# Attention chunks of groups 2 to 5 served two at a visit, in a fused attention and MLP kernel

## The chip, the cores and the metric

The kernel runs on one core of a Trainium2 chip. The metric is the device time of one execution in microseconds (us), lower is better. The core's engines each run their own instruction queue in order and meet through semaphores: TensorE (PE, with its weight loads PEld), VectorE (DVE), ScalarE (ACT), GpSimd (POOL) and SyncE (SP). SP and POOL issue the DMAs here. PE writes into PSUM, which the kernel uses as eight banks of 128 partitions x 512 floats.

## The reference

Attention with a decay for each head, over 4 batches, 8 heads, 768 positions and a head size of 64, in blocks of 64 positions with a running state; its output, as 3072 tokens of 512, goes through an MLP with an exact GELU and a hidden size of 2048.

```python
for b in range(nb):                                   # blocks of 64 positions
    intra = einsum('bhic,bhjc->bhij', qb, kb) * Dmask  # lam**(i-j) where i >= j
    intra = einsum('bhij,bhjd->bhid', intra, vb)
    inter = einsum('bhid,bhde->bhie', qb * lam_pow, kv_state)
    out[:, :, sl] = intra + inter
    kv_state = lam_block * kv_state + einsum('bhsd,bhse->bhde', kb * rev_pow, vb)
x = out.transpose(0, 2, 1, 3).reshape(3072, 512)
h = x @ w_in
return (0.5 * h * (1 + erf(h / sqrt(2)))) @ w_out
```

## The kernel before

**Chunks and groups.** The kernel takes 128 positions at a time. Chunk n is positions 128 (n // 4) onwards of batch n % 4, all eight heads; there are 24 chunks. Four chunks, one of each batch at the same positions, are a group of 512 tokens; there are six groups, 0 to 5. The MLP works on one group while attention prepares the next, so "in group 1" means: while the MLP of group 1 runs and chunks 8 to 11 are prepared.

**What a chunk needs.**

- Loads of k, q and v (`load`, line 67), issued by POOL, cast on the way from float32 to bf16. `prefetch` keeps them four chunks ahead of the scores; the buffers (10 for k, 8 for q and v) come free when the older chunk has been used.
- `begin` and `dma_transposes` (lines 188 and 189): SP issues two DMA transposes, k to kT and q to qT. Both have three buffers, so those of chunk n wait for chunk n - 3: kT for its scores, qT for the first part of its outputs.
- `decay_v` (line 163): POOL scales v by powers of the decay, into v_dec (7 buffers).
- `scores` (line 196): eight matmuls on PE, each on 64 of the array's 128 rows, into two banks of the tag "sc"; then `masked` (line 204) on DVE, two multiplications by the causal mask, PSUM to SBUF (sc_m).
- `outputs`: the part from the states (line 226, four matmuls on the whole array) and the part from the values (line 231, eight matmuls on 64 of the array's columns) into the bank "o"; then DVE scales it into x_t (line 241), the MLP's input.
- `next_state` (line 211): four matmuls into the bank "t", and two DVE operations (lines 218 and 219), once in each group for each of its own chunks.

**The MLP.** In groups 1 to 5 it is 30 blocks of about equal length. Blocks 0 to 15 each make one slice of 128 hidden units (four matmuls of 512 columns into a bank "mh", line 412, then GELU on ACT, line 416). Blocks 16 to 29 multiply by w_out in seven products of half size, two blocks each, in the order m3, m4, m5, m2, m1, m6, m7 (sixteen matmuls for two blocks, line 306). m3, m4, m5 and m2 take a bank "mo" each in turn, m1 takes two "mh" (called s and r), m6 writes s and m7 adds to r. DVE forms sums of the inputs (g_sum, line 281) and of the results; SP stores the two halves of a group's output after m6 and m7 (line 316). The tags sc, mh and mo have two banks each, o and t one.

**The order.** It is written out by hand. PE, DVE, ACT, POOL and SP get their instructions in the order in which the Python code calls for them. The list `todo` holds pairs of a place and a step: place(g + f) is a share f of group g's blocks, and a step runs before the first block whose start is at or after its place. In the kernel before, chunk i of the next group (i from 0 to 3) has its scores at 0.21 + 0.2 i in group 1 and at 0.06 + 0.245 i in groups 2 to 4; its outputs at the place of the next chunk's scores, just ahead of them, and those of the last chunk at 0.93; its `begin` 0.32 ahead of its scores (0.28 for chunk 8). So a visit is outputs of one chunk, then scores of the next. The states of a group's own chunks stand at 0.01, 0.12, 0.18 and 0.24.

Of the kernel before, what the change touches and what calls it, by code (L numbers as in the profile page):

```python
# [8 lines left out]
F32 = mybir.dt.float32  # L9
BF16 = mybir.dt.bfloat16  # L10
# [5 lines left out]
def kernel(  # L16
# [23 lines left out]
    M = 4  # L40
    NG = NCH // M
# [7 lines left out]
    work_pool = ctx.enter_context(tc.tile_pool(name="work", bufs=3))  # L49
# [115 lines left out]
    def transposed(c, name, tag, empty):  # L165

        src, t_ps = getattr(c, name), bank([128, HP, C], BF16, tag, "t_ps")
        for hp in range(HP):
            nc.tensor.transpose(t_ps[:, hp, :], src[:, 2 * hp:2 * hp + 2, :], ident)  # L169
        dst = work_pool.tile([128, HP, C], BF16, tag=name + "T", name=name + "T")  # L170
        setattr(c, name + "T", dst)
        empty(dst, t_ps)  # L172

# [3 lines left out]
    def transposes(c):  # L177
        if c.early:
            transposed(c, "k", "mo", nc.scalar.copy)
            transposed(c, "q", "mo", nc.vector.tensor_copy)  # L180
        else:
            transposed(c, "k", "mh", nc.scalar.copy)
            transposed(c, "q", "mh", scaled)

    def dma_transposes(c):
        c.kT = work_pool.tile([128, HP, C], BF16, tag="kT", name="kT")
        c.qT = work_pool.tile([128, HP, C], BF16, tag="qT", name="qT")
        nc.sync.dma_start_transpose(out=c.kT, in_=c.k.rearrange("p h d -> p (h d)"))
        nc.sync.dma_start_transpose(out=c.qT, in_=c.q.rearrange("p h d -> p (h d)"))

    def scores(c):
        sc_ps = [bank([128, HP, C], F32, "sc", f"sc_ps{hi}") for hi in range(2)]
        for hp in range(HP):
            for hi in range(2):
                p = slice(hi * D, (hi + 1) * D)
                nc.tensor.matmul(sc_ps[hi][:, hp, :], c.kT[p, hp, :], c.qT[p, hp, :], start=True, stop=True)  # L196
        c.sc_m = work_pool.tile([128, HP, 2, C], BF16, tag="sc_m", name="sc_m")
        c.sc_ps = sc_ps
        for hi in range(0 if c.n == 0 else 2):
            masked(c, hi)  # L200

    def masked(c, hi):
        mask = decay[:, hi] if c.early else cmask[:, None, :].to_broadcast((128, HP, C))
        nc.vector.tensor_mul(c.sc_m[:, :, hi, :], c.sc_ps[hi], mask)  # L204

    def next_state(c):
        if c.sb == NB - 1:
            return
        kv_ps = bank([128, HP, 128], F32, "t", "kv_ps")
        for hp in range(HP):  # L210
            nc.tensor.matmul(kv_ps[:, hp, :], c.k[:, 2 * hp:2 * hp + 2, :], c.v_dec[:, 2 * hp:2 * hp + 2, :],  # L211
                             start=True, stop=True)
        new = work_pool.tile([128, HP, 128], BF16, tag="state_f", name="state", bufs=8)
        if c.sb == 0:
            nc.vector.tensor_mul(new, kv_ps, lam_blk)
        else:
            tmp = work_pool.tile([128, HP, 128], F32, tag="tmp", name="tmp")
            nc.vector.tensor_add(tmp, kv_ps, states[c.n])  # L218
            nc.vector.tensor_mul(new, tmp, lam_blk)  # L219
        states[c.n + M] = new  # L220

    def outputs(c, x_t, off, evacuate=True):
        o_ps = bank([128, HP, C], F32, "o", "o_ps")
        if c.sb > 0:
            for hp in range(HP):
                nc.tensor.matmul(o_ps[:, hp, :], states[c.n][:, hp, :], c.qT[:, hp, :],  # L226
                                 start=(hp == 0), stop=False, skip_group_check=True)
        v = c.v if c.early else c.v_dec
        for hi in range(2):
            for hp in range(HP):  # L230
                nc.tensor.matmul(o_ps[hi * D:(hi + 1) * D, hp, :], v[:, 2 * hp + hi, :], c.sc_m[:, hp, hi, :],  # L231
                                 start=(c.sb == 0 and hp == 0), stop=True, skip_group_check=True)
        c.x_o, c.o_ps = x_t[:, :, off * C:(off + 1) * C], o_ps
        if evacuate:
            empty_outputs(c)

    def empty_outputs(c):
        if c.n < 2 * M:
# [222 lines left out]
    live = {}  # L461
# [10 lines left out]
    def early(n):  # L472
        live[n] = begin(n, early=True)
        return live[n]
# [9 lines left out]
    c = early(0)  # L484
# [4 lines left out]
    causal(1)  # L489
    keep_warm(2)  # L490
    scores(c)
    for hi in range(2):
        masked(c, hi)
# [5 lines left out]
    outputs(live[0], xT[0], 0)  # L499
# [5 lines left out]
    outputs(live[1], xT[0], 1)  # L505
    c = early(2)
    transposed(c, "k", "mh", copy)
    transposed(c, "q", "mo", copy)
# [31 lines left out]
    x1 = lambda n: outputs(live[n], xT[1], n - M)  # L540
# [4 lines left out]
    e = N1  # L545
    group0 = {
        1: [lambda: scores(live[2])],
        5: [lambda: outputs(live[2], xT[0], 2)],
        6: [lambda: next_state(live[0])],
        7: [lambda: next_state(live[1])],  # L550
        8: [lambda: both_transposed(live[3])],
        9: [lambda: next_state(live[2])],
        10: [lambda: scores(live[3])],
        12: [lambda: outputs(live[3], xT[0], 3)],
        17: [lambda: next_state(live[3])],
        e: [w_out_sums, lambda: decay_v(live[4], nc.vector)],
        e + 8: [lambda: transposes(live[4])],
        e + 9: [lambda: scores(live[4])],
        e + 10: [lambda: x1(4), lambda: transposes(live[5])],
        e + 11: [lambda: scores(live[5])],  # L560
        e + 12: [lambda: x1(5), lambda: transposes(live[6])],
        e + 13: [lambda: scores(live[6])],
        e + 14: [lambda: x1(6), lambda: transposes(live[7])],
        e + 15: [lambda: scores(live[7])],
    }
# [10 lines left out]
    todo.sort()  # L576

    def step(minus_kind, n):
        kind = -minus_kind
        if kind == BEGIN:  # L580
            live[n] = begin(n)
            dma_transposes(live[n])
            decay_v(live[n], nc.gpsimd)
        elif kind == SCORES:
            scores(live[n])
            prefetch(n + M)
        elif kind == STATE:
            next_state(live[n])
        else:
            outputs(live[n], xT[n // M], n % M)  # L590

    done = 0
    for g in range(NG):
        if g + 1 < NG:
            alloc_x(g + 1)
        for i, (run, cost) in enumerate(mlp_blocks(g)):
            if g == 0:
                for act in group0.get(i, []):
                    act()
            while todo and todo[0][0] <= done:  # L600
                step(*todo.pop(0)[1:])
            run()
            done += cost
        for item in [t for t in todo if t[2] // M == g + 1 and t[1] != -STATE]:
            todo.remove(item)
            step(*item[1:])


# [28 lines left out]
```

## Time and profile before

| what | value |
|---|---|
| median of three runs | 209.67 us (209.66 to 209.96) |
| the profiled execution | 209.99 us |
| its span, first to last instruction | 208.2 us |
| granted TensorE clock, mean | 0.998 |
| group 1 begins, group 2, group 3, group 4 | 53.50, 84.87, 115.96, 147.06 us |
| h blocks (line 412), matmuls of 512 columns | 75.3 us in 318, start to start 0.216 us |
| scores (line 196) | 9.5 us in 192 |
| outputs (lines 226 and 231, groups 1 to 5) | 7.7 us in 80 and 9.3 us in 160 |
| masks of groups 1 to 5 (line 204) | 25.6 us in 40 |
| kT and qT by DMA, issue to landing | least 2.4, median 5.8 and 5.2, most 8.3 and 9.0 us |

The span is what the profiler saw from the first to the last instruction; the time of the execution has some 1.8 us around it. [...] DMA landings are told by semaphores.

### The profile page before, as it was taken

The numbers are of one execution on the slowest core, as the hardware profiler recorded it, in microseconds if no ns is written. First come the engines' busy times: TensorE is split into PE (matmuls) and PEld (weight loads), VectorE is DVE, ScalarE is ACT, GpSimd is POOL, SyncE is SP. The second block draws the span as 40 slices with busy tenths as digits, with TensorE's granted clock in tenths as the row PEclk, the third lists the DMA queues.
The fourth block names the chain that finished last, engine by engine and source line by source line (L and its number), as shares of the span: only waits on it lengthen the run. The fifth ranks groups of instructions, "written<-read, shape, count | busy, mean of one in ns | idle before, by whom it ended". The sixth has DMA issues, their size and how long they took to land.

```text
span 208.2 us, 4142 instructions
## 1 busy us (share of the span) xinstructions
PE 200.3 (96%) x1708; PEld 130.5 (63%) x1725; DVE 139.0 (67%) x220; ACT 81.7 (39%) x145; POOL 97.1 (47%) x112
## 2 busy tenths in 40 slices
PE   7889999999999999999999999999999999999992
PEld 2457574465555788654688554688555688544881
DVE  4744525855476789889779689579678579123482
ACT  4966563324555410265420265410365410466200
POOL 8999953799998995499300493000200000000000
PEclk9999999999999999999999999999999999999999
DMA  5999999999999999999930699100651000500014
GB/s 116 155 174 177 200 207 188 154 215 148 151 177 154 153 150 154 233 141 175 155 25 3 219 134 175 29 0 3 227 103 29 0 0 3 201 0 0 3 50 151
DMA packets 102370, 24.65 MB, mean 118 GB/s; under 512 B 92880, under 2 KB 99536, under 8 KB 102352
## 3 DMA queue, kind: packets, MB, share of 16 engines
q0 software_dynamic: 80688, 13.37, 90.2%
q1 hardware_dynamic: 21664, 11.02, 23.5%
q8 instruction: 13, 0.21, 0.4%
q14 instruction: 5, 0.04, 0.1%
HBM read 27.27 MB, written 6.29 MB: 161 GB/s over the span
## 4 chain that ended last, share of the span: by engine, by line
PE 86%; POOL 8%; DVE 3%; issue 1%; POOLq 0%; DVEq 0%
PE h_ps L412 39%; PE p_ps L306 9%; PE r_ps L306 8%; PE q_ps L306 8%; PE o_ps L426 7%; PE o_ps L231 4%; PE s_ps L306 3%; PE sc_ps L196 3%; PE kv_ps L211 3%; POOL w_in_t L88 3%; PE o_ps L226 2%; POOL k_t L67 2%; POOL q_t L67 2%; POOL v_t L67 2%; PE t_ps L169 1%
## 5 line engine op out<-in xcount | busy, mean ns | idle before, releaser
L416 ACT ACTIVATE g_t<-h_ps 128x512 bf16<-128x512 f32 (+2 forms) x101 | 58.2, 576 | 81.2 <-PE h_ps L412 81.0
L412 PE MATMUL h_ps<-x_t,w_in_t 128*128 128x512 bf16 (+3 forms) x446 | 88.7, 343 | 0.6
L412 PEld LDWEIGHTS <-w_in_t 128*128 128x128 bf16 x460 | 40.2, 98 | 36.0 <-issue 0.6
L163 POOL TENSOR_TENSOR v_dec<-v_t,lam_m 128x512 bf16<-128x512 bf16 x23 | 25.2, 1101 | 44.5 <-PE kv_ps L211 42.9
L306 PEld LDWEIGHTS <-g_sum 128*128 128x128 bf16 x400 | 38.6, 98 | 5.2
L281 DVE TENSOR_TENSOR g_sum<-g_t 128x1024 bf16<-128x1024 bf16 x50 | 33.6, 716 | 11.3 <-ACT g_t L416 11.3
L204 DVE TENSOR_TENSOR sc_m<-sc_ps,cmask 128x512 bf16<-128x512 f32 x40 | 25.6, 680 | 2.0 <-PE sc_ps L196 2.0
L67 POOL DMA_DIRECT2D v_t<-in_v_dram x24 | 21.4, 893 | 3.3 <-DMA w_out_t<-in_moe_w_out_dram 2.9
L67 POOL DMA_DIRECT2D k_t<-in_k_dram x24 | 22.2, 924 | 1.7 <-DMA w_out_t<-in_moe_w_out_dram 1.4
L67 POOL DMA_DIRECT2D q_t<-in_q_dram x24 | 21.6, 898 | 2.1 <-DMA w_out_t<-in_moe_w_out_dram 2.1
L306 PE MATMUL r_ps<-w_sum,g_sum 128*128 128x256 bf16 x160 | 19.3, 273 | 0.1
L241 DVE TENSOR_TENSOR x_t<-o_ps,lam_q 128x512 bf16<-128x512 f32 x16 | 11.0, 687 | 10.2 <-PE o_ps L231 10.2
L306 PEld LDWEIGHTS <-g_t 128*128 128x128 bf16 x160 | 15.3, 98 | 3.2
L218 DVE TENSOR_TENSOR tmp<-kv_ps,state 128x512 f32<-128x512 f32 x16 | 11.0, 689 | 7.8 <-PE kv_ps L211 7.8
L426 PE MATMUL o_ps<-w_out_t,g_t 128*128 128x512 bf16 x61 | 14.8, 380 | 0.1
L219 DVE TENSOR_TENSOR state<-tmp,lam_blk 128x512 bf16<-128x512 f32 x16 | 14.4, 901 | 0.5
L306 PE MATMUL p_ps<-w_sum,g_t 128*128 128x256 bf16 x80 | 10.1, 273 | 0.0
L196 PE MATMUL sc_ps<-qT,kT 64*128 64x128 bf16 x192 | 9.5, 218 | 0.3 <-DVE qT L172 0.3
L306 PE MATMUL q_ps<-w_sum,g_t 128*128 128x256 bf16 x80 | 9.7, 273 | 0.0
L470 PE MATMUL idle_ps<-idle 128*128 128x256 bf16 (+1 forms) x33 | 8.4, 393 | 1.2 <-DVE idle L101 1.2
L426 PEld LDWEIGHTS <-g_t 128*128 128x128 bf16 x64 | 5.8, 98 | 6.1
L306 PE MATMUL p_ps<-w_out_t,g_sum 128*128 128x256 bf16 x80 | 9.6, 273 | 0.0
(65 smaller groups left out, 168.0 us busy)
## 6 DMA issues: line engine op xcount, KB each, us to landing
out_dram<-o_sb SPq DMA_DIRECT2D x9, 512.0 KB, 2.8
k_t<-in_k_dram POOLq DMA_DIRECT2D x24, 128.0 KB, 5.9
q_t<-in_q_dram POOLq DMA_DIRECT2D x24, 128.0 KB, 6.1
v_t<-in_v_dram POOLq DMA_DIRECT2D x24, 128.0 KB, 6.2
w_out_t<-in_moe_w_out_dram POOLq DMA_DIRECT2D x4, 512.0 KB, 11.1
w_in_t<-in_moe_w_in_dram POOLq DMA_DIRECT2D x7, 256.0 KB, 7.5
out_dram<-o_sb SPq DMA_DIRECT2D x5, 256.0 KB, 5.7
wide_w<-in_moe_w_in_dram SPq DMA_DIRECT2D x1, 512.0 KB, 4.2
```

Source lines behind the costliest of these rows:

```text
L67: nc.gpsimd.dma_start(raw[n, name], chunk_of(name, n))
L163: eng.tensor_mul(c.v_dec, c.v, lam_m[:, :, None].to_broadcast((128, H, D)))
L196: nc.tensor.matmul(sc_ps[hi][:, hp, :], c.kT[p, hp, :], c.qT[p, hp, :], start=True, stop=True)
L204: nc.vector.tensor_mul(c.sc_m[:, :, hi, :], c.sc_ps[hi], mask)
L218: nc.vector.tensor_add(tmp, kv_ps, states[c.n])
L219: nc.vector.tensor_mul(new, tmp, lam_blk)
L241: nc.vector.tensor_mul(c.x_o, c.o_ps, lam_q)
L281: nc.vector.tensor_tensor(gsum[i][:, ks, :], g_t[:, ka + k:ka + k + n4, ta], g_t[:, kb + k:kb + k + n4, tb], op=op)
L306: nc.tensor.matmul(o, left[i](k, slice(u * C, (u + 1) * C)), right[i](k), start=(begin and k == 0), stop=(k == KH - 1), skip_group_check=True)
L412: nc.tensor.matmul(h_ps[:, k, lo:hi], w_in_t[:, ki, (kf + k) * 128:(kf + k + 1) * 128], x_t[:, ki, cols.start + lo:cols.start + hi], start ...
L416: nc.scalar.activation(g_t[:, kf:kf + ks, cols], h_ps, ACT.Gelu)
L426: nc.tensor.matmul(om[io], g_t[:, kf, io * C:(io + 1) * C], w_out_t[:, kf, :], start=(kf == 0), stop=(kf == NK2 - 1))
```

## The change

Nothing is computed in another way: the same matmuls, masks and transfers are called in another order and into other banks.

- `visit(when, done, asked, banks, masks)` replaces the separate steps. It runs the outputs of up to two chunks (`done`): the part from states for both, then the part from values for both, then both evacuations. The second chunk's outputs go to the bank "t". Then it runs the scores of up to two further chunks (`asked`): the first in "sc", the second in "mo" (in "mh" at one visit); the masks of the second chunk come first, unless `masks` gives each of the four masks a place of its own.
- In group 1 there is a visit before block 8 (scores of 8 and 9), one before block 20 (outputs of 8 and 9, scores of 10 and 11) and one before block 26 (outputs of 10 and 11, scores of 12 and 13, which belong to group 3). In groups 2 and 3 there is a visit before block 9 (outputs of the group's first two chunks, scores of the other two) and one before block 26 (outputs of these, scores of the first two of the group after). In group 4 they are the same without the scores of the last.
- At the visits before block 26 the masks stand at blocks 26 and 28 and at blocks 1 and 2 of the next group.
- The begins move: chunk 8 stays at 0.93 of group 0; 9, 10 and 11 stand at 1.0, 1.13 and behind the visit before block 8 of group 1; 12 and 13 at 1.57 and 1.60; and in the later groups the last two chunks at 0.0 and 0.04, the first two of the group after at 0.57 and 0.60.
- qT has four buffers in place of three.

```diff
-        qT = work_pool.tile([128, HP, C], BF16, tag="qT", name="qT")
+        qT = work_pool.tile([128, HP, C], BF16, tag="qT", name="qT", bufs=4)
...
-    def outputs(c, x_t, off, evacuate=True):
-        o_ps = bank([128, HP, C], F32, "o", "o_ps")
+    def from_states(c, tag):
+        c.o_ps = bank([128, HP, C], F32, tag, "o_ps")
...
+    def outputs(*chunks):
+
+        for c, tag in zip(chunks, ("o", "t")):
+            from_states(c, tag)
+        for c in chunks:
+            from_values(c)
+        for c in chunks:
             empty_outputs(c)
...
-    BEGIN, STATE, SCORES, OUTPUTS = 0, 1, 2, 3
-    todo = [(total, -OUTPUTS, 2 * M - 1)]
-    for n in range(2 * M, NCH):
-        g, i = n // M - 1, n % M
-        first, apart = (0.21, 0.2) if g == 1 else (0.06, 0.245)
-        at = first + apart * i
-        todo += [(place(g + at - (0.28 if n == 2 * M else 0.32)), -BEGIN, n), (place(g + at), -SCORES, n),
-                 (place(g + (at + apart if i < M - 1 else 0.93)), -OUTPUTS, n)]
-    todo += [(place(n // M + (0.01, 0.12, 0.18, 0.24)[n % M]), -STATE, n) for n in range(M, NCH - M)]
...
+    def begin_at(when, n):
+        def run():
             live[n] = begin(n)
             dma_transposes(live[n])
             decay_v(live[n], nc.gpsimd)
...
+    def visit(when, done, asked, banks="mo mo", masks=None):
+
+        def run():
+            outputs(*[live[n] for n in done])
+            for n, tags in zip(asked, ("sc sc", banks)):
+                scores(live[n], tags, mask=False)
+            if masks is None:
+                for n in reversed(asked):
+                    for hi in range(2):
+                        masked(live[n], hi)
+            for n in asked:
+                prefetch(n + M)
+        at(when, run)
+        if masks:
+            for w, (n, hi) in zip(masks, [(n, hi) for n in asked for hi in range(2)]):
+                at(w, lambda n=n, hi=hi: masked(live[n], hi))
+
+    B = 1 / (NK2 + 14)
+    for g in range(1, NG - 1):
+        n = (g + 1) * M
+        for i, w in enumerate((0.01, 0.12, 0.18, 0.24)):
+            at(g + w, lambda i=i, g=g: next_state(live[g * M + i]))
+        if g == 1:
+            for i, w in enumerate((-0.07, 0.0, 0.13)):
+                begin_at(g + w, n + i)
+            visit(g + 8 * B, [], [n, n + 1])
+            begin_at(g + 8 * B, n + 3)
+            visit(g + 20 * B, [n, n + 1], [n + 2, n + 3], banks="mh mh")
         else:
+            for i in (2, 3):
+                begin_at(g + (i - 2) * 0.04, n + i)
+            visit(g + 9 * B, [n, n + 1], [n + 2, n + 3])
+        later_on = [n + M, n + M + 1] if g < NG - 2 else []
+        for i, c_n in enumerate(later_on):
+            begin_at(g + 0.57 + 0.03 * i, c_n)
+        visit(g + 26 * B, [n + 2, n + 3], later_on, masks=(g + 26 * B, g + 28 * B, g + 1 + 1 * B, g + 1 + 2 * B))
```

More of the change, by code (lines that the diff above doesn't have):

```diff
@@ L186, in dma_transposes, with scores @@
         c.kT = work_pool.tile([128, HP, C], BF16, tag="kT", name="kT")
-        c.qT = work_pool.tile([128, HP, C], BF16, tag="qT", name="qT")
+        c.qT = work_pool.tile([128, HP, C], BF16, tag="qT", name="qT", bufs=4)
         nc.sync.dma_start_transpose(out=c.kT, in_=c.k.rearrange("p h d -> p (h d)"))
         nc.sync.dma_start_transpose(out=c.qT, in_=c.q.rearrange("p h d -> p (h d)"))
-    def scores(c):
-        sc_ps = [bank([128, HP, C], F32, "sc", f"sc_ps{hi}") for hi in range(2)]
+    def scores(c, tags="sc sc", mask=True):
+        sc_ps = [bank([128, HP, C], F32, tag, f"sc_ps{hi}") for hi, tag in enumerate(tags.split())]
         for hp in range(HP):
@@ L198, in scores @@
         c.sc_ps = sc_ps
-        for hi in range(0 if c.n == 0 else 2):
+        for hi in range(2 if mask else 0):
             masked(c, hi)
@@ L220, in next_state, with from_values @@
         states[c.n + M] = new
[L222 to L223 removed]
+    def from_states(c, tag):
+        c.o_ps = bank([128, HP, C], F32, tag, "o_ps")
         if c.sb > 0:
             for hp in range(HP):
[L226 removed]
+                nc.tensor.matmul(c.o_ps[:, hp, :], states[c.n][:, hp, :], c.qT[:, hp, :],
                                  start=(hp == 0), stop=False, skip_group_check=True)
+    def from_values(c):
         v = c.v if c.early else c.v_dec
@@ L230, in outputs @@
             for hp in range(HP):
-                nc.tensor.matmul(o_ps[hi * D:(hi + 1) * D, hp, :], v[:, 2 * hp + hi, :], c.sc_m[:, hp, hi, :],
+                nc.tensor.matmul(c.o_ps[hi * D:(hi + 1) * D, hp, :], v[:, 2 * hp + hi, :], c.sc_m[:, hp, hi, :],
                                  start=(c.sb == 0 and hp == 0), stop=True, skip_group_check=True)
-        c.x_o, c.o_ps = x_t[:, :, off * C:(off + 1) * C], o_ps
-        if evacuate:
+    def outputs(*chunks):
[4 more added lines that the diff above has]
+        for c in chunks:
             empty_outputs(c)
     def empty_outputs(c):
+        off = c.n % M
+        c.x_o = xT[c.sb][:, :, off * C:(off + 1) * C]
         if c.n < 2 * M:
@@ L498 @@
     transposed(c, "q", "mo", copy)
-    outputs(live[0], xT[0], 0)
+    outputs(live[0])
     nc.scalar.copy(w_in_t[:, :, :256], wide_w)
@@ L504 @@
     make_lam_blk()
-    outputs(live[1], xT[0], 1)
+    outputs(live[1])
     c = early(2)
@@ L547 @@
         1: [lambda: scores(live[2])],
-        5: [lambda: outputs(live[2], xT[0], 2)],
+        5: [lambda: outputs(live[2])],
         6: [lambda: next_state(live[0])],
@@ L553 @@
         10: [lambda: scores(live[3])],
-        12: [lambda: outputs(live[3], xT[0], 3)],
+        12: [lambda: outputs(live[3])],
         17: [lambda: next_state(live[3])],
@@ L558, with at @@
         e + 9: [lambda: scores(live[4])],
-        e + 10: [lambda: x1(4), lambda: transposes(live[5])],
+        e + 10: [lambda: outputs(live[4]), lambda: transposes(live[5])],
         e + 11: [lambda: scores(live[5])],
-        e + 12: [lambda: x1(5), lambda: transposes(live[6])],
+        e + 12: [lambda: outputs(live[5]), lambda: transposes(live[6])],
         e + 13: [lambda: scores(live[6])],
-        e + 14: [lambda: x1(6), lambda: transposes(live[7])],
+        e + 14: [lambda: outputs(live[6]), lambda: transposes(live[7])],
         e + 15: [lambda: scores(live[7])],
     }
-    BEGIN, STATE, SCORES, OUTPUTS = 0, 1, 2, 3
-    todo = [(total, -OUTPUTS, 2 * M - 1)]
-    for n in range(2 * M, NCH):
-        g, i = n // M - 1, n % M
-        first, apart = (0.21, 0.2) if g == 1 else (0.06, 0.245)
-        at = first + apart * i
-        todo += [(place(g + at - (0.28 if n == 2 * M else 0.32)), -BEGIN, n), (place(g + at), -SCORES, n),
-                 (place(g + (at + apart if i < M - 1 else 0.93)), -OUTPUTS, n)]
-    todo += [(place(n // M + (0.01, 0.12, 0.18, 0.24)[n % M]), -STATE, n) for n in range(M, NCH - M)]
[L576 to L580, printed above, removed]
+    todo = []
+    def at(when, run):
+        todo.append((place(when), run))
+    def begin_at(when, n):
+        def run():
             live[n] = begin(n)
@@ L583, in step @@
             decay_v(live[n], nc.gpsimd)
[L584 to L588, printed above, removed]
-        else:
-            outputs(live[n], xT[n // M], n % M)
+        at(when, run)
[10 more added lines that the diff above has]
+                prefetch(n + M)
+        at(when, run)
+        if masks:
[12 more added lines that the diff above has]
+            visit(g + 20 * B, [n, n + 1], [n + 2, n + 3], banks="mh mh")
+        else:
+            for i in (2, 3):
[5 more added lines that the diff above has]
+        visit(g + 26 * B, [n + 2, n + 3], later_on, masks=(g + 26 * B, g + 28 * B, g + 1 + 1 * B, g + 1 + 2 * B))
+    at(1.0, lambda: outputs(live[2 * M - 1]))
+    todo.sort(key=lambda t: t[0])
     done = 0
@@ L600 @@
             while todo and todo[0][0] <= done:
-                step(*todo.pop(0)[1:])
+                todo.pop(0)[1]()
             run()
             done += cost
-        for item in [t for t in todo if t[2] // M == g + 1 and t[1] != -STATE]:
-            todo.remove(item)
-            step(*item[1:])
+    assert not todo
 _INS = ['q', 'k', 'v', 'lam', 'moe_w_in', 'moe_w_out']
```

5 lines of the change are left out of this document (1 added, 4 removed).

## The prediction

> **What bounds the kernel now.** I read the page's busy times and its chain first, then where TensorE (PE) loses time.
>
> ```profile
> PE 200.3 (96%) x1708; PEld 130.5 (63%) x1725; DVE 139.0 (67%) x220; ACT 81.7 (39%) x145; POOL 97.1 (47%) x112
> PE 86%; POOL 8%; DVE 3%; issue 1%; POOLq 0%; DVEq 0%
> ```
>
> PE is busy for 96% of the span and is 86% of the chain. So a PE microsecond saved between 53.5 us (start of group 1's blocks) and the end comes off the time, and one waited there is added; VectorE (DVE), at 67%, counts only where it makes PE wait. Next the timeline of PE around one visit of the old kind (outputs of chunk 12, then scores of chunk 13), with one state product from the chain:
>
> ```profile
> 94.83 0.39 PE L226 MATMUL o_ps<-qT,state 128*128 128x128 bf16 x4
> 95.15 0.42 PE L231 MATMUL o_ps<-sc_m,v_dec 128*64 128x128 bf16 x8
> 95.50 0.40 PE L196 MATMUL sc_ps<-qT,kT 64*128 64x128 bf16 x8
> 95.83 1.04 PE L412 MATMUL h_ps<-x_t,w_in_t 128*128 128x512 bf16 x4
> ...
> 91.09 0.22 PE kv_ps L211 x4
> ```
>
> Columns: start, length, engine and line. Four full-array matmuls of 128 columns take 0.22 us (last line). The four at L226 use the full array, the eight at L231 half its columns (128*64), the eight at L196 half its rows (64*128); the eights run two at a time, so 0.22 us would do for each as well. But the starts are 0.32, 0.35 and 0.33 us apart. The excess is 0.10 + 0.13 + 0.11 = 0.34 us for three changes of array form, 0.113 us each. PE waits for nobody there.
>
> **Part 1, the changes of form (removed).** The old schedule has, in each of the four groups it prepares, scores alone (2 changes), three visits of outputs with scores (3 each) and outputs alone (2): 13, in all 52. The new one has two of scores of two chunks (2), then a full visit before block 20 and one before block 26 (3 each) in group 1, so 8; 6 in group 2; 6 in group 3; and 3 + 2 in group 4: 25. (Chunks 12 and 13 are asked for in group 1, and so on; the matmuls are the same.) 27 changes fewer, 27 x 0.113 = 3.05 us of PE. All of it is on the path.
>
> **Part 2, what the earlier scores need.** Scores wait for kT and qT, which SyncE (SP) makes by DMA transposes. The old schedule asks for one chunk at a time, 6 to 7 blocks apart; the new one asks for the second right behind the first. SP's timeline, and the landing of its 55.43 issue:
>
> ```profile
> 52.17 1.59 SPq L431 DMA_DIRECT2D out_dram<-o_sb  x2
> 53.87 1.37 SPq L188 DMA_TRANSPOSE kT<-k_t  x1
> 55.43 1.88 SPq L189 DMA_TRANSPOSE qT<-q_t  x1
> ...
> DMA to landing us min/median/max: 9.0/9.0/9.0
> ```
>
> These two transposes are chunk 9's, queued behind group 0's last two stores. In the new order of SP they still are: their begin moves from 1.09 to 1.0 group, still behind those stores. So qT of chunk 9 lands at 55.43 + 9.0 = 64.4 us. Their company is unchanged as well: the loads in flight until then were issued before either schedule's first visit.
>
> When does PE ask? Its timeline before the first visit:
>
> ```profile
> 59.67 0.81 PE L412 MATMUL h_ps<-x_t,w_in_t 128*128 128x512 bf16 x3
> 60.41 0.40 PE L196 MATMUL sc_ps<-qT,kT 64*128 64x128 bf16 x8
> 60.74 1.04 PE L412 MATMUL h_ps<-x_t,w_in_t 128*128 128x512 bf16 x4
> 61.61 0.28 PE L211 MATMUL kv_ps<-v_dec,k_t 128*128 128x128 bf16 x2
> ```
>
> Scores of chunk 8 leave 60.41 (0.42 us with two changes), so the state product begins at 61.2, scores of 8 at 61.5 and of 9 at 61.7. **First wait: 64.4 - 61.7 = 2.7 us** (2.4 to 3.0 if the transfers vary by 0.3). PE is in order: the sixteen h blocks, the products and everything later move back with it.
>
> **Part 3, the same in groups 2 and 3.** There chunks 14 and 15 (18 and 19) begin at the group's start, behind the two output stores of the group before. Group 3's start in the old trace is 115.96 us, and SP then reads:
>
> ```profile
> 114.45 2.80 SPq L316 DMA_DIRECT2D out_dram<-o_sb  x2
> 117.37 1.39 SPq L188 DMA_TRANSPOSE kT<-k_t  x1
> 118.88 1.20 SPq L189 DMA_TRANSPOSE qT<-q_t  x1
> 120.18 1.21 SPq L188 DMA_TRANSPOSE kT<-k_t  x1
> 121.50 1.27 SPq L189 DMA_TRANSPOSE qT<-q_t  x1
> ...
> DMA to landing us min/median/max: 5.3/5.3/5.3
> ```
>
> The last line is that of the 121.50 issue. In the new order these four slots are the two chunks', so the second qT lands at 121.50 + 5.3 = 126.8, 10.8 us into the group (group 2: begins at 84.87; 90.55 + 5.1, 10.8 too). PE's arrival at those scores: nine h blocks at 4 x 0.216 us, 7.77; four state products, 0.89; states of two chunks and a change, 0.54; values of two, 0.58; scores of the first with the changes around, 0.25: 10.0 us. **Wait 0.8 us in each of groups 2 and 3.** With a lone transfer (2.4 us, the qT issued at 153.0) it would be none; with the 6.7 us of group 1's qT at 66.57 it would be 2.2. The rows of the same slots decide. In group 4 no loads run, the fourth slot would land at 8.4 us, and there is no wait.
>
> **Part 4, before block 26 of group 1.** The new visit there asks for chunks 12 and 13. qT12 waits until the states of chunk 8 at block 20 have read its buffer (four buffers for qT, so chunk n waits for outputs of n - 4), and kT13 for scores of 10 in the same visit. So SP issues qT12 0.25 us after that visit's start, kT13 and qT13 1.36 us apart (the pitch of 66.57 and 67.93): qT13 at +3.0. PE is at its scores at +8.25 (1.66 for the visit, six product blocks at 0.87, 1.36 into the next). It waits if qT13 takes over 5.3 us. Group 1's own rows say 6.6 to 6.7 (1.4 us of wait), with loads issued without a break; group 2's, 5.1 to 5.2 (none). The new GpSimd (POOL) order issues loads in two bursts of two chunks with a lull before, which lies between; I take 0.7, and keep 0 to 2.6.
>
> **Part 5, cover elsewhere.** DVE does the same evacuations and masks. Its tightest place is again group 1's products: two evacuations and four masks at its 0.60 us pitch keep it 3.6 us from the visit before block 20; the mh banks come free first (the masks of the second chunk go first), 2 us before m1 wants them, and the mo banks of chunk 13's scores at about the moment when PE comes. The old 0.2 us wait there (outputs at 82.58 took 0.54 us to the next product in place of 0.35) goes. If that cover fails, see the fourth rival. The t bank, shared with the state products, comes free some 0.15 us before the second outputs want it. POOL's loads and v_dec come 5 us or more ahead of use.
>
> **Sum.** 2.7 + 0.7 + 0.8 + 0.8 - 3.05 - 0.2 = +1.75 us. The profiled execution took 209.99 (span 208.2); the median is 209.67, 0.3 less, so the change is put on the median: 211.4 us. By the ends of the unknown waits the sum runs from 2.4 - 3.25 = -0.85 to 3.0 + 2.6 + 2 x 1.6 - 3.05 = +5.75, 1.6 being twice the wait of part 3.
>
> **Rivals.** *The later waits vanish; only the first is left.* With PE 2.7 us late while POOL and the transfers run on, the traffic beside the later transposes may be thinner: group 4's slots show 2.4 us. The sum is then 2.7 - 3.25 = -0.55, 209.1 us. It decides when the three later waits total under 0.55 us. Against it: POOL, too, waits for the state products before its loads, so they move along with PE. 0.20.
>
> *No wait at all, 206.4 us.* That needs qT9 by 61.7, 6.3 us after its issue. If the two busy DMA queues shared evenly, it would take twice a lone one's 2.4 us, and land at 60.2. The 9.0 us row is of the very transfer, and speaks against it. 0.05. [...]
>
> *The clock falls in the pause.* The granted clock here:
>
> ```profile
> 207.30:208.20 0.90, 0.00 (x0) 0.00 (x0) 0.00 (x0) 0.00 (x0) 0.00 (x0) 0.50 0.00 0
> ```
>
> The third figure from the end is the clock: 0.50, after the last matmul ended at 204.4, so 2.9 us of rest were enough; the pause is 2.7. At the kernel's start the 512-column matmuls were 0.43 us apart for some 4.2 us in place of 0.22: a loss of 2.1 us, 213.5 in all. 0.10. [...]
>
> *DVE becomes the bound in group 1's products.* One g_sum at 77.48 took 1.40 us, not 0.68, beside a v_dec on POOL; one or two such in the full queue push the mo banks and r late by 0.7 to 1.4: 212.4 us. 0.08.
>
> **Numbers.** Forecast 211.4 with chance 0.57, its own range 210.3 to 213.0; rivals 0.20, 0.05, 0.10, 0.08. The measurement can tell 0.2%, 0.42 us. The first rival's 209.1 is near that edge: of its 0.20, 0.13 is faster and 0.07 the same; with the second, faster is 0.18; slower 0.57 + 0.10 + 0.08 = 0.75. The range for 8 in 10 is 209.0 to 213.4.
>
> **What would show it.** Right: a gap of some 2.7 us on PE between the two chunks' scores at 61.7 us, ended by the DMA of qT; gaps of 0.8 us at the second scores of the visits 10 us into groups 2 and 3, and one before block 26 of group 1; changes of form still at 0.10 us. Wrong: scores of chunk 9 that follow without a gap, or a wait at DVE or a lower clock in the chain in its place.

## The result and the profile after

The changed kernel takes 217.89 us, the median of four executions (217.17, 217.36, 218.42 and 222.4), beside 209.81 us for the kernel before in the same comparison. The ratio is 1.0356, with a 95% interval of 1.0284 to 1.0429, and leaves out the execution of 222.4 us, the slow one: the kernel is slower, by some 7.5 us, over four times the forecast loss of 1.75. The profiled execution is the one of 222.4 us (span 220.6). Its mean granted clock is 0.969, that of the other three 0.992, 0.992 and 0.984; why they differ is told below.

The page of the changed kernel, its busy times, the first numbers of its chain, and the granted clock in 40 slices of 5.5 us:

```profile
PE 203.9 (92%) x1708; PEld 133.1 (60%) x1725; DVE 139.7 (63%) x220; ACT 81.7 (37%) x145; POOL 98.5 (45%) x112
PE 35%; DMA 24%; POOL 23%; issue 16%; DVE 0%; POOLq 0%
...
PEclk9999999999979999799799999699999999999999
```

PE's share fell from 96% to 92%. The chain now leaves PE at a late transfer, goes back through loads and POOL, and does not return: its shares say that a DMA ended the last stall, not that DMA carries 24% of the work. In the last line four slices of the middle show a 7 or a 6, where the clock was lower for part of the slice.

PE's timeline at the four visits that ask for two chunks right behind each other, when the second is not there (columns: start, length, engine, line, form, count, and in brackets the idle time and what ended it):

```profile
61.36 0.40 PE L196 MATMUL sc_ps<-qT,kT 64*128 64x128 bf16 x8
63.70 0.61 PE L196 MATMUL sc_ps<-qT,kT 64*128 64x128 bf16 x8 [1.94 <-DMA qT<-q_t]
64.24 2.31 PE L422 MATMUL h_ps<-x_t,w_in_t 128*128 128x512 bf16 x5
...
84.12 0.40 PE L196 MATMUL sc_ps<-qT,kT 64*128 64x128 bf16 x8
86.50 0.40 PE L196 MATMUL sc_ps<-qT,kT 64*128 64x128 bf16 x8 [1.99 <-DMA qT<-q_t]
...
101.81 0.40 PE L196 MATMUL sc_ps<-qT,kT 64*128 64x128 bf16 x8
104.90 0.61 PE L196 MATMUL sc_ps<-qT,kT 64*128 64x128 bf16 x8 [2.69 <-DMA qT<-q_t]
...
136.50 0.40 PE L196 MATMUL sc_ps<-qT,kT 64*128 64x128 bf16 x8
138.91 0.61 PE L196 MATMUL sc_ps<-qT,kT 64*128 64x128 bf16 x8 [2.02 <-DMA qT<-q_t]
```

Each pair is one chunk's eight scores and the next chunk's. Start to start less the 0.22 us that eight matmuls need, the four pauses are 2.12, 2.16, 2.87 and 2.19 us, 9.34 in all. All four are ended by the DMA transpose of qT, and nothing else makes PE wait in the body. Group 4's visit has no loads beside it, and its transposes land in 2.4 to 3.2 us; it has no pause.

The third line shows a second cost. Five matmuls of 512 columns start within 2.31 us, where they are 0.216 us apart elsewhere. The windows behind the first and the last pause, with one of undisturbed work between (columns: the window and its length; busy time and count of PE, its weight loads, DVE, ACT and POOL; then the granted clock, the DMA share and GB/s):

```profile
64.00:67.20 3.20, 2.98 (x13) 1.13 (x11) 2.88 (x5) 0.60 (x1) 2.16 (x3) 0.52 2.12 168
67.20:84.00 16.80, 16.80 (x170) 12.55 (x168) 12.90 (x19) 5.35 (x9) 11.72 (x14) 1.00 1.39 109
139.00:142.60 3.60, 3.60 (x17) 1.47 (x17) 3.07 (x6) 0.60 (x1) 0.00 (x0) 0.56 1.15 145
```

The clock was 0.52 and 0.56 in the outer ones, 1.00 between. The trace's clock records give four stretches of 3.41 us at 0.50 in the body, from 63.69, 87.58, 104.64 and 138.78 us. The second begins 1.1 us after its pause has ended (86.50), the others 0.01 to 0.26 us before theirs end. PE is busy for 3.15 to 3.41 us of each, so each costs some 3.41 x 0.5 = 1.7 us, 6.8 together.

The account of the profiled execution: 209.99 before, less the 3.25 forecast for fewer changes of form and one old wait, plus 9.34 of pauses, plus 6.8 at half clock: 222.9, beside 222.4 measured. By estimate one stretch lowers the mean clock of a 218 us run by 1.7 / 218 = 0.008, so 0.992, 0.992 and 0.984 mean one, one and two; at which places is not on record. Without 1.7 us for each, the four executions are 215.0 to 215.7 us: some 9 us of pauses in all of them, and between one and four falls of the clock.

### The profile page after: what moved, and what is told of

Same layout as the page of the kernel before. It is cut to its first block, busy times and chain, and to the rows that moved or that the text cites. A ratio compares the mean times of both kernels' runs of the same rounds, so it can differ in the third digit from the quotient of the medians.

```text
span 220.6 us, 4142 instructions
## 1 busy us (share of the span) xinstructions
PE 203.9 (92%) x1708; PEld 133.1 (60%) x1725; DVE 139.7 (63%) x220; ACT 81.7 (37%) x145; POOL 98.5 (45%) x112
## 4 chain that ended last, share of the span: by engine, by line
PE 35%; DMA 24%; POOL 23%; issue 16%; DVE 0%; POOLq 0%
PE h_ps L422 16%; DMA v_t<-in_v_dram 12%; POOL k_t L67 6%; POOL v_dec L163 5%; POOL q_t L67 5%; PE r_ps L316 5%; PE q_ps L316 5%; PE p_ps L316 5%; DMA w_out_t<-in_moe_w_out_dram 5%; POOL v_t L67 5%; DMA qT<-q_t 3%; DMA q_t<-in_q_dram 3%; PE s_ps L316 2%; POOL w_in_t L88 2%; DMA k_t<-in_k_dram 1%
## 5 line engine op out<-in xcount | busy, mean ns | idle before, releaser
L422 PE MATMUL h_ps<-x_t,w_in_t 128*128 128x512 bf16 (+3 forms) x446 | 91.7, 353 | 0.8 <-issue 0.2
L422 PEld LDWEIGHTS <-w_in_t 128*128 128x128 bf16 x460 | 41.6, 100 | 40.0 <-issue 6.5
L163 POOL TENSOR_TENSOR v_dec<-v_t,lam_m 128x512 bf16<-128x512 bf16 x23 | 26.9, 1193 | 57.3 <-PE kv_ps L211 50.0
L291 DVE TENSOR_TENSOR g_sum<-g_t 128x1024 bf16<-128x1024 bf16 x50 | 34.6, 738 | 18.5 <-ACT g_t L426 18.5
L316 PEld LDWEIGHTS <-g_sum 128*128 128x128 bf16 x400 | 39.6, 100 | 5.7
L316 PEld LDWEIGHTS <-g_t 128*128 128x128 bf16 x160 | 15.7, 98 | 2.9
L196 PEld LDWEIGHTS <-kT 64*128 64x128 bf16 x192 | 6.2, 98 | 12.7 <-issue 8.2
L316 PE MATMUL s_ps<-w_sum,g_sum 128*128 128x256 bf16 x80 | 10.6, 291 | 0.0
L354 DVE TENSOR_TENSOR o_sb<-f_e,p_ps 128x512 f32<-128x512 f32 x5 | 3.4, 686 | 11.1 <-issue 8.3
L316 PE MATMUL q_ps<-w_out_t,g_sum 128*128 128x256 bf16 x80 | 9.6, 273 | 0.0
```

Source lines behind the costliest of these rows:

```text
L163: eng.tensor_mul(c.v_dec, c.v, lam_m[:, :, None].to_broadcast((128, H, D)))
L291: nc.vector.tensor_tensor(gsum[i][:, ks, :], g_t[:, ka + k:ka + k + n4, ta], g_t[:, kb + k:kb + k + n4, tb], op=op)
L316: nc.tensor.matmul(o, left[i](k, slice(u * C, (u + 1) * C)), right[i](k), start=(begin and k == 0), stop=(k == KH - 1), skip_group_check=True)
L422: nc.tensor.matmul(h_ps[:, k, lo:hi], w_in_t[:, ki, (kf + k) * 128:(kf + k + 1) * 128], x_t[:, ki, cols.start + lo:cols.start + hi], start ...
```

## The experiments

**The second chunk's scores read the first chunk's kT and qT.** This takes away what the pauses wait for and leaves the order, the banks and the transfers.

```diff
-                nc.tensor.matmul(sc_ps[hi][:, hp, :], c.kT[p, hp, :], c.qT[p, hp, :], start=True, stop=True)
+                nc.tensor.matmul(sc_ps[hi][:, hp, :], of.kT[p, hp, :], of.qT[p, hp, :], start=True, stop=True)
...
-                scores(live[n], tags, mask=False)
+                scores(live[n], tags, mask=False, of=live[asked[0]])
```

> At each visit the second chunk's scores read kT and qT of the first chunk, so they do not wait for their own transposes (which are still issued); the scores of every second chunk are therefore of another chunk. Theory (the lost time is waits for the second chunk's transposes and the clock that falls in them; the fewer changes of array form are a real gain): no pause over 0.5 us on PE between 60 and 180 us, clock as before, 209.7 - 3.05 - 0.2 = 206.4 us (205.8 to 207.2). Rival (the wider visits themselves cost: banks in mo, mh and t, and the masks queued on DVE): the excess stays, 213 us or more, with PE waiting for DVE. Second rival (the fewer changes of form bring nothing): 209.5 us.

Median 208.05 us of five executions, ratio to before 0.9921 (0.9892 to 0.9950), clock 1.0 throughout the body. (One of the five took 515.05 us, which nothing on record explains; the ratio leaves it out, and the other four took 207.5 to 209.13.) PE's timeline at group 1's first visit and at group 2's:

```profile
61.35 0.62 PE L197 MATMUL sc_ps<-qT,kT 64*128 64x128 bf16 x16
...
93.70 0.66 PE L234 MATMUL o_ps<-sc_m,v_dec 128*64 128x128 bf16 x16
95.56 0.62 PE L197 MATMUL sc_ps<-qT,kT 64*128 64x128 bf16 x16 [1.20 <-DMA qT<-q_t]
```

Sixteen scores now run as one. One pause is left, before group 2's scores, for the first chunk's own qT: 1.86 us start to start, where the changed kernel has 0.60 between the same two (101.21 and 101.81 us), so 1.26. 208.05 - 1.26 = 206.8: the fewer changes of form, with the old wait that went, save 209.7 - 206.8 = 2.9 us. So the saving is as forecast, and all that was lost, the clock too, hangs on the transposes of the second chunks.

**The last two begins of groups 2 and 3 ahead of the stores of the group before.**

```diff
             for i in (2, 3):
-                begin_at(g + (i - 2) * 0.04, n + i)
+                begin_at(g - 4 * B, n + i)
```

> In groups 2 to 4 the begins of the last two chunks stand right behind the visit before block 26 of the group before, so their four transposes are issued ahead of the two output stores. Theory (these transposes are late because they stand behind the stores): the waits of 2.9 and 2.2 us at the first visits of groups 2 and 3 vanish, with their falls of the clock; those of group 1 stay: 217.3 - 5.0 = 212.3 us, down to 210.5 where a fall of the clock goes with them. Rival (they are late because of the loads that run beside them, wherever they stand): at least half of these waits stays, 214.5 us or more.

Seven of eleven executions took 209.69 to 211.33 at a clock of 0.997 to 1.0, and four 215.1 to 216.1 at 0.984; the median of all is 211.1, and the ratio of those in which the clock held is 1.0032 (1.0009 to 1.0055). The profiled one is of the four. Groups 2 and 3 have no pause in it, as expected. But the visit before block 26 of group 1 has two, and SP's timeline shows where the second comes from:

```profile
85.09 0.40 PE L196 MATMUL sc_ps<-qT,kT 64*128 64x128 bf16 x8 [0.64 <-DMA qT<-q_t]
88.50 0.61 PE L196 MATMUL sc_ps<-qT,kT 64*128 64x128 bf16 x8 [3.01 <-DMA qT<-q_t]
```

```profile
76.72 3.31 SPq L189 DMA_TRANSPOSE qT<-q_t  x1
80.14 1.21 SPq L188 DMA_TRANSPOSE kT<-k_t  x1
81.44 1.23 SPq L189 DMA_TRANSPOSE qT<-q_t  x1
...
92.92 2.13 SPq L326 DMA_DIRECT2D out_dram<-o_sb  x2
```

The first line is qT of chunk 12, whose issue alone took 3.31 us, where the changed kernel's took 1.22. So qT of chunk 13 was issued at 81.44 in place of 79.18. It landed 6.9 us later, no slower than the 7.2 of the changed kernel, and the wait grew to 3.2 us. The begins of chunks 14 and 15, issued behind it and ahead of the stores at 92.92, did not lengthen its landing; why the issue at 76.72 took so long the trace doesn't say. The seven executions fit two cured places and group 1's two pauses as they were: 209.7 - 3.25 + 2.12 + 2.16 = 210.7. The edit cures two places; that it worsens a third is not shown beyond this one execution.

**Idle matmuls in the pauses.** Nine of 512 columns, some 2 us, between the scores of the first chunk and those of 9, 13, 15 and 19; the scores overwrite them.

```diff
+        for _ in range(fill):
+            nc.tensor.matmul(sc_ps[0].rearrange("p h c -> p (h c)"), idle[:, :128], idle, start=True, stop=True)
...
-                scores(live[n], tags, mask=False)
+                scores(live[n], tags, mask=False, fill=9 if n in (9, 13, 15, 19) else 0)
```

> Nine matmuls of 512 columns of zeros (1.94 us) stand ahead of the second chunk's scores at the four visits where PE waited; their result is overwritten. The transposes come no earlier. Theory (part of the loss is the clock that falls to half for 3.41 us in the pauses): the granted clock stays at its value of before (0.998), PE still spends 9.3 us in the four places, all runs agree within 0.5 us: 209.7 - 3.25 + 9.3 + 4 x 0.1 for two more changes of form = 216.2 us, and the profiled run, too, near 216. Rival (the pause alone counts, and the clock costs nothing in the runs that count): 217.3 us as the changed kernel or up to 0.5 more, with the same spread of 1.2 us and more between runs.

Median 217.54 us. The profiled execution had a clock of 0.853 on average, 240.76 us, so its trace says nothing of the pauses; the others were at 1.0 (216.45 to 218.01). The same kernel was taken once more:

> The kernel of e3_fill once more, for a profile with the clock undisturbed. Theory: the granted clock does not fall between 10 and 200 us; the fill of 1.94 us and what is left of each pause add up to the pauses of the changed kernel (9.3 us, less or more by 2 as the landings vary), and no matmul runs at 0.427 us behind them; 216.0 to 217.5 us against 217.2 to 222.4 for the changed kernel. Rival: the clock falls behind the fills as well.

Median 216.9 us (216.33 to 218.39), ratio 1.0343 (1.0308 to 1.0379), clock 0.998 to 1.0 in all four. The first visit:

```profile
61.38 0.40 PE L198 MATMUL sc_ps<-qT,kT 64*128 64x128 bf16 x8
61.71 2.12 PE L194 MATMUL sc_ps<-idle 128*128 128x512 bf16 x9
63.76 0.40 PE L198 MATMUL sc_ps<-qT,kT 64*128 64x128 bf16 x8
64.09 2.12 PE L424 MATMUL h_ps<-x_t,w_in_t 128*128 128x512 bf16 x8
```

Behind the filled pause eight h matmuls take 2.12 us, where five took 2.31 behind the empty one. With PE busy for some 2 us of each pause the clock held (0.998 to 1.0) in seven of the eight executions of this kernel, all but that of 240.76 us, where the changed kernel's four had 0.969 to 0.992. So here the falls went with PE's standing idle. With the clock held, start to start less 0.22 is 2.16, 2.15, 2.43 and 3.04 us at the four places, 9.8 in all, and 209.7 - 3.25 + 9.8 = 216.3 beside 216.55 for that execution. At the first two places that is the fill itself with its two changes of form (9 x 0.216 + 0.22 = 2.16), at the other two a wait for qT is left behind it. Pauses of this length alone make the kernel some 7 us slower, and the clock adds 1.7 for each fall. By the times the fill wins little: 217.54 and 216.9 us beside the changed kernel's 217.17 to 218.42. The expectation that all executions agree within 0.5 us missed: with the clock held they still lie 1.6 and 2.1 us apart, so the waits themselves vary.

**More buffers.** kT five, qT six; tmp one in place of its own number, to make room.

```diff
-        c.kT = work_pool.tile([128, HP, C], BF16, tag="kT", name="kT")
-        c.qT = work_pool.tile([128, HP, C], BF16, tag="qT", name="qT", bufs=4)
+        c.kT = work_pool.tile([128, HP, C], BF16, tag="kT", name="kT", bufs=5)
+        c.qT = work_pool.tile([128, HP, C], BF16, tag="qT", name="qT", bufs=6)
...
-            tmp = work_pool.tile([128, HP, 128], F32, tag="tmp", name="tmp")
+            tmp = work_pool.tile([128, HP, 128], F32, tag="tmp", name="tmp", bufs=1)
```

> Five buffers for kT and six for qT in place of three and four (and one for tmp in place of three, to make room). Theory (before block 26 of group 1 PE waits 2.15 us because the transposes of chunks 12 and 13 wait for buffers that the visit before block 20 frees): that wait vanishes, the other three stay: 217.3 - 2.15 = 215.1 us, down to 213.4 where a fall of the clock goes with it. Rival (those transposes wait for their loads or lie behind other traffic): the wait stays at 1.5 us or more and the time within 0.7 us of 217.3.

Median 217.25 us, ratio 1.0330 (1.0271 to 1.0389): by the time alone, nothing. But the trace shows PE before block 26 of group 1, and SP's issue of chunk 13's transposes:

```profile
83.33 0.67 PE L196 MATMUL sc_ps<-qT,kT 64*128 64x128 bf16 x16
```

```profile
70.91 1.19 SPq L188 DMA_TRANSPOSE kT<-k_t  x1
72.21 1.21 SPq L189 DMA_TRANSPOSE qT<-q_t  x1
```

The sixteen scores run as one: qT13 is issued at 72.21, in place of 79.18. That pause was the buffers', as the prediction had it. The other three stay (1.83, 2.18 and 2.68 us), and the clocks of the four executions (0.992, 0.984, 0.968, 0.976) mean, by the same estimate, one to four falls; less 1.7 us each they are 211.5 to 214.2, 1 to 4 us under the changed kernel's. The expectation on the time missed because it took the falls for fixed.

**The first visit of group 1 before block 11** in place of 8 (one execution).

```diff
-            visit(g + 8 * B, [], [n, n + 1])
+            visit(g + 11 * B, [], [n, n + 1])
```

> Only group 1's first visit moves, from before block 8 to before block 11 (2.6 us later). Theory (qT of chunk 9 lands at a time of its own, about 63.7 us, whenever PE asks): the pause at that visit falls from 2.1 us to under 0.5, the other three stay at 2 to 3 us, the time falls by 2.1 to 3.8 (with one fall of the clock less). Rival (the transfer is held up by what PE does, so that the wait moves with the visit): a pause of 1.5 us or more there.

219.49 us. The pause at the moved visit is gone, as expected, and so is group 1's other one; but the time did not fall, because group 2's visit pays:

```profile
63.93 0.62 PE L196 MATMUL sc_ps<-qT,kT 64*128 64x128 bf16 x16
...
99.12 0.61 PE L196 MATMUL sc_ps<-qT,kT 64*128 64x128 bf16 x8 [4.58 <-DMA qT<-q_t]
101.52 0.61 PE L196 MATMUL sc_ps<-qT,kT 64*128 64x128 bf16 x8 [1.78 <-DMA qT<-q_t]
```

Here both chunks are late, 6.4 us together, and the clock is at 0.50 for all of the 6.75 us from 98.15 to 104.90. PE comes to this visit 7.3 us earlier than in the changed kernel (values at 93.88, there 101.21), but qT of chunk 14, though issued 5.4 us earlier, takes 9.6 us in place of 5.8. In this execution a pause that was removed alone came back at the next place of the same kind.

**The loads put apart** (one execution). At the first visits of groups 2 and 3 the loads that the second chunk asks for move behind two v_dec in POOL's queue.

```diff
-            for n in asked:
+            late = done and asked and asked[-1] % M == M - 1 and asked[0] > 3 * M
+            for n in asked[:1] if late else asked:
                 prefetch(n + M)
         at(when, run)
+        if done and asked and asked[-1] % M == M - 1 and asked[0] > 3 * M:
+            at(when + 0.31, lambda: prefetch(asked[-1] + M))
```

> In groups 2 and 3 the loads asked for by the second chunk at the first visit come behind two v_dec in POOL's queue, which wait for state products at blocks 4 and 6; so the loads no longer come as six in a row. Theory (the landings of the second chunk's transposes came 1.5 to 2 us later than the old trace's rows because of that burst of loads): the pauses in groups 2 and 3 fall from 2.9 and 2.2 to 0.8 to 1.5 us. Rival (four transposes in a row are enough to delay the last): they stay at 2 us or more.

**Chunks 19 to 23 not loaded** (one execution).

```diff
+        if n > 18:
+            raw[n, name] = kept[name]
+            return
```

> Chunks 19 to 23 are not loaded; they use the q, k and v of chunk 18 (and tmp has one buffer to make room), so in group 3 no loads run beside the transposes, and in group 2 only chunk 18's. Theory (loads set how long a transpose takes): the four transposes at the start of group 3 land 2.4 to 3.3 us after their issue and the pause there is gone; in group 2 it falls from 2.9 to 0.5 to 1.5 us; those of group 1 stay. Rival (transposes in a row crowd each other without loads too): group 3's pause stays at 1 us or more.

211.67 us and 210.91 us, with no fall of the clock in either body. POOL's timeline while the transposes of chunks 14 and 15 run, in the kernel before and in the changed one:

```profile
89.00 0.88 POOL L67 DMA_DIRECT2D v_t<-in_v_dram  x1
89.89 1.06 POOL L163 TENSOR_TENSOR v_dec<-v_t,lam_m 128x512 bf16<-128x512 bf16 x1
90.88 0.93 POOL L67 DMA_DIRECT2D k_t<-in_k_dram  x1
```

```profile
96.13 0.88 POOL L67 DMA_DIRECT2D v_t<-in_v_dram  x1
96.99 0.91 POOL L67 DMA_DIRECT2D k_t<-in_k_dram  x1
97.87 0.90 POOL L67 DMA_DIRECT2D q_t<-in_q_dram  x1
```

Before, each chunk's three loads are followed by a v_dec of 1.06 us; after, six loads follow each other, because `visit` asks for both chunks' loads at once. The landing of the qT in the fourth slot (SP's 97.53 issue in the changed kernel, and its like), and the pause that it ends:

| kernel | group 2: landing, pause | group 3: landing, pause |
|---|---|---|
| before, same slots | 5.1, none | 5.3, none |
| changed | 7.3, 2.87 | 6.7, 2.19 |
| loads apart | 5.6, 1.13 | 4.8, 0.37 |
| loads left out | 5.1, 0.71 | 2.5, none |

The landings with the loads apart are within 0.5 us of those of before. Other traces say the same. The fourth slot took 6.5 to 7.5 us in the five further ones whose loads come in one row, as the changed kernel's do (the first experiment, both with idle matmuls, more buffers, and the moved visit in group 3). In group 3 of the next three kernels it took 7.5 with the loads in a row, 4.6 and 5.3 with them apart. With no loads at all (group 3 of the last row) it is 2.5, so it is the loads beside them that lengthen the transposes' landings. An estimate from these 2.5 us, that two queues sharing evenly land it in twice that, is 5.0 us, and the trace, with 6.7 to 7.3 beside a full row of loads, does not agree. Group 1's pauses, which neither edit touches, were 1.67 and 1.13 us with the loads apart, 1.85 and 1.49 with loads left out, and 2.12 and 2.16 in the changed kernel: they vary by up to 1.0 from execution to execution. So the differences between the last two rows prove little; the 1.7 and 1.8 us between the changed kernel and the loads apart are beyond that, and the idle matmuls' 2.43 and 3.04, with no fall of the clock either, stand on the changed kernel's side.

**All the edits together.** Begins ahead of the stores, more buffers, and the first visit before block 11:

> All three cures together: the begins of the last two chunks ahead of the stores, five and six buffers for kT and qT, and group 1's first visit before block 11 in place of 8. Theory (the whole loss is second chunks' transposes that come late): no pause over 0.5 us on PE from 60 to 180 us, clock near 1.0, 206.4 to 207.2 us, faster than both kernels by 1.2% or more. Rival (the transposes of two chunks always crowd each other, and the wait only moves on): a pause of 1 us or more at some visit and 208.5 us or more.

208.58 us, the median of twelve executions, ratio 0.9941 (0.9920 to 0.9962). That is faster than the kernel before, but by half of what was expected: no wait for a qT is left in the body, but two for DVE came up, 0.4 us before chunk 13's scores and 0.6 at a state product of group 2. The same with the loads apart, and then with the first visit before block 12:

> The three cures (begins ahead of the stores, more buffers, group 1's first visit before block 11) and the loads of groups 2 and 3 spread as in e7. Theory: the pauses of 0.6 and 0.8 us that were left with the cures alone go, 207.0 us (206.4 to 207.6). Rival (what is left is loads and transposes that share the DMA engines in groups 1 and 2 however they are ordered): 208.0 to 209.0 us.

> As e9_all_spread with group 1's first visit before block 12. Theory: chunk 9's qT, which lands near 63.7 us in every run, has 0.9 us more; within 0.3 us of e9_all_spread if its first visit never waits, else faster by up to 0.5 us.

208.29 us (ratio 0.9931, 0.9907 to 0.9955) and 208.44 us (0.9930, 0.9912 to 0.9949): both faster than the kernel before by 0.7%, and not to be told apart, nor from 208.58. So the 207.0 us expected of the loads apart did not come; 208.29 lies in its rival's range. The page of the version with 208.29, and what its scores still wait for:

```profile
PE 197.9 (96%) x1708; PEld 130.7 (63%) x1725; DVE 139.0 (67%) x220; ACT 81.8 (40%) x145; POOL 97.5 (47%) x112
PE 82%; POOL 8%; DVE 4%; DMA 3%; issue 1%; POOLq 0%; SPq 0%
```

```profile
PE sc_ps L196 <- DMA qT<-q_t: 0.5, 1, 0.5
```

PE is back at 96%, and 82% of the chain. Two pauses remain, some 0.6 us in group 1, put down to DVE, and 0.7 in group 2, the row above; 209.7 - 2.9 + 1.3 = 208.1, and the profiled execution took 208.2.

## Why the prediction was wrong

The direction, the mechanism and the saving were right; the time lay some 4 us above the upper end of the range, 213.4.

- **Part 1, changes of form: right.** 3.05 + 0.2 forecast, 2.9 shown by the kernel whose second scores need no transfer of their own.
- **Part 2, the first wait: right, a little large.** 2.7 forecast, 2.12 measured. qT of chunk 9 was issued at 55.50, as forecast behind the stores, and took 8.2 us in place of the 9.0 of the old trace; PE was there at 61.7.
- **Part 3, groups 2 and 3: the step that failed.** "The rows of the same slots decide" gave 0.8 us in each; 2.87 and 2.19 came. PE was at the second scores 10.0 us into group 2 (102.03 less 92.01), as forecast; what was off is the landing, 7.3 and 6.7 us. The slots are the same in SP's queue, but their company isn't: the old 5.1 and 5.3 us were measured beside loads with a v_dec between, and the new order puts two chunks' loads into those same microseconds. The burst was named in part 4 and not followed into part 3. With the loads apart the old landings are back. The 6.7 us row that the part had as its other end, 2.2 us of wait, was the one to take.
- **Part 4, before block 26 of group 1: the mechanism right, the size wrong.** "I take 0.7, and keep 0 to 2.6": it was 2.16. The step 5.3 us held: qT13 took 7.2, 1.9 more. The buffers as cause are shown by the kernel with more of them.
- **Part 5, DVE: right.** In the changed kernel PE waits for DVE nowhere in the body. Only in the last kernels, with the transfers moved, do waits for DVE appear, of 0.4 to 0.7 us, before chunk 13's scores or at a state product.
- **The rivals.** Thinner traffic behind the first wait, 0.20, was the opposite of what came: it was denser. The fall of the clock, 0.10, is the other term that was mis-sized. It was priced as one fall that excludes the other cases, when it can follow each pause and adds to it: at 1.7 us each it came at all four pauses of one execution, and the mean clock of the others allows one or two. Four pauses near 2 us should have carried it in the sum.
- **The range.** By the ends of its unknown waits the sum ran to +5.75, which is 215.4 us, and the waits alone gave 215.0 to 215.7. The range for 8 in 10 stopped at 213.4, and no term of the sum had the clock, which is what lies above.

Of the 7.5 us, then: some 9 of pauses, where 5.0 were forecast, less 3.25, plus one fall of the clock at 1.7, or two. The difference from the forecast is some 4 us of waits (2.07 + 1.39 + 1.46 - 0.58 = 4.3 in the profiled execution) and 1.7 to 3.4 of clock.

Open is why the pauses of group 1 differ by up to a microsecond between executions of kernels that agree there, and what would take away the last 0.6 to 0.7 us in groups 1 and 2.

## What to carry to other kernels

Serving two chunks at a visit saves changes of array form, here 0.11 us each, but the second chunk is then needed a visit earlier, and all that feeds it has to move along: its place in the transfer queue, its buffers, and what else loads at that moment; with these moved the change gained 0.7% in place of losing 3.6%. A landing time read from the old trace was that of the transfer's old company, and 5.1 and 5.3 us became 7.3 and 6.7 beside loads in one row: when a change moves other transfers beside it, take the slow row. Behind each of the four pauses of 2.12 to 2.87 us in the changed kernel's trace the clock was at half for 3.41 us: price such a pause with the 1.7 us that may follow it, and each pause on its own.

## What the hardware showed that was not expected

The clock fell after shorter rests than the 2.9 us at the end of the old trace. The empty pauses of PE between two chunks' scores in the bodies of the traces of the changed kernel and of the edits taken alone (start to start less 0.22 us), and the clock behind them:

| kernel | half clock behind it | full clock behind it |
|---|---|---|
| changed | 2.12, 2.16, 2.87, 2.19 | none |
| begins ahead of the stores | 2.03, 3.19 | none |
| more buffers | 2.68 | 1.83, 2.18 |
| first visit before block 11 | 2.65 | none |
| loads apart | none | 1.67, 1.13, 1.13, 0.37 |
| loads left out | none | 1.85, 1.49, 0.71 |

A fall lasted 3.41 us in the changed kernel; with the two pauses in a row of the moved visit, which the table leaves out, the clock was at 0.50 for 6.75 us at least. In the changed kernel's other executions the mean clock allows, by the estimate above, only one or two falls, so the same pause doesn't bring one each time. The kernel with more buffers shows both cases (columns as above: window, length, PE busy, then the other engines; the third figure from the end is the clock):

```profile
95.05:98.47 3.42, 2.58 (x41) 1.83 (x40) 3.09 (x5) 1.19 (x2) 3.42 (x4) 1.00 1.89 153
98.47:101.88 3.41, 2.25 (x17) 1.12 (x17) 1.83 (x4) 0.60 (x1) 3.41 (x5) 1.00 1.77 179
101.88:105.29 3.41, 3.41 (x17) 1.57 (x16) 3.41 (x6) 2.39 (x4) 2.75 (x3) 1.00 2.26 174
...
129.19:132.60 3.41, 0.96 (x25) 0.74 (x25) 1.62 (x3) 0.22 (x1) 2.22 (x2) 1.00 2.21 161
132.60:136.01 3.41, 3.36 (x15) 1.36 (x15) 2.74 (x5) 0.60 (x1) 0.00 (x0) 0.50 1.36 139
```

Behind the pause of 2.18 us (scores at 97.23 and 99.63) the clock holds at 1.00; behind that of 2.68 (129.75 and 132.65) the next 3.41 us have 0.50. What decides whether a pause of some 2 us costs a fall is not shown: 2.18 us did not here, and 2.16 and 2.19 did in the changed kernel's trace.

Kernels with pauses of some 2 us also spread more (with the clock held, too, as the idle matmuls show): the one with the begins ahead of the stores took 209.7 to 211.3 us or 215.1 to 216.1, while the kernel before, run beside it, stayed between 209.69 and 210.32.
